# Seven block products in the second MLP product of a fused attention and MLP kernel

## The chip, the core and the metric

The kernel runs on one core of a Trainium2 chip. The metric is the device time of one execution in microseconds (us): a median of 360.05 over 3 runs (360.02 to 360.05). Five engines work side by side, each on its own queue of instructions in order: TensorE (PE, matmuls), VectorE (DVE), ScalarE (ACT), GpSimd (POOL) and SyncE (SP, which only issues DMAs here). Sums of matmuls are kept in PSUM, which has eight banks of 128 x 512 f32; all other tiles are in SBUF.

## What is computed

```python
scores = scale * q @ k^T + decay          # 8 batches x 8 heads, 576 positions, head size 64; causal
attn   = softmax(scores)
x      = (attn @ v), heads side by side   # 4608 tokens x 512
h      = x @ w_in                         # 512 -> 2048
g      = h - tanh(h)
out    = g @ w_out                        # 2048 -> 512, f32
```

`decay` is the difference of two running sums of log f.

## The kernel before

**Attention** goes by pairs of heads: 8 batches of 4 pairs make 32 pairs, `p` = 0 to 31, in a loop with one more turn for what trails. A pair has seven score tiles (`TILES`, 0 to 6; tile 3 is the small one, 128x128, the others up to 128x512). For each, `scores` runs matmuls into one of two PSUM banks (`ps_sc`, line 286), ScalarE takes the exponential into SBUF (`e`, for tile 3 `el`, line 295), and GpSimd clears what lies above the diagonal (line 305). A pair's product with v (`values`, line 317) runs in the following pair, after its tile 2; VectorE divides by the row sums (`rs`, `xn`, lines 324 to 326), and `turn` has two DMA transposes on SyncE's queue (lines 340 and 342) write the result to `XR`, the MLP's input, after tile 3.

**q and k** must have the head's dimension on partitions. The first three batches are transposed on TensorE (`trans`, line 224) and copied by VectorE. From batch `FAR` = 3 on, GpSimd issues loads of blocks of 128 positions (`load_block`, line 86), SyncE issues five DMA transposes into `TQ` and five into `TK` (`turn_block`, line 91), and four copies each of 64 x 1152 (`place`, line 94) move them to `QT` and `KT`, of which there are two sets that take turns by batch. The table `LOADS` says after which tile of which pair each of these is issued; `p0` is the first pair of the batch before the one that is loaded.

**The MLP** goes by nine units of 512 tokens. A step of `mlp1` is four matmuls of 512 columns into a PSUM bank (line 356), tanh on ScalarE (361), and an addition on VectorE that writes `gt`, g in 16 bits (364). There are 16 such steps, one for each 128 of the 2048 columns. A step of `mlp2` is four of the 16 matmuls of 512 columns that make 128 tokens of output (372); after the fourth, ScalarE copies the bank to `ost` (376) and SyncE stores it (378). A unit has 16 steps of each kind. Both use `ps_m`, a ring of three banks; `ps_av` has two, `ps_tr`, for transposes, one.

**The order.** For all engines but ScalarE the program's order is the queue's order (`manual_schedule`). ScalarE's order is free after the start: a scheduler sets it when the kernel is built. The main loop puts MLP steps between the attention's steps, by `take` steps a pair, spread evenly:

```python
take = 0 if p < NPAIR else 2 if p == NPAIR else 7 if p == NPAIR + 1 else 6 if p <= 2 * NPAIR else 8
```

What is left when attention ends (some two units) runs alone at the end.

Of the kernel before, what the change touches and what calls it, by code (L numbers as in the profile page):

```python
# [8 lines left out]
FP32 = mybir.dt.float32  # L9
FP16 = mybir.dt.float16  # L10
# [7 lines left out]
FAR = 3  # L18
# [3 lines left out]
def kernel(  # L22
# [23 lines left out]
    NFT = DFF // P  # L46
    NCH = DM // P
    UW = 512
    NU = NT // UW

    cst = ctx.enter_context(tc.tile_pool(name="cst", bufs=1))
# [1 line left out]
    wpl = ctx.enter_context(tc.tile_pool(name="wpl", bufs=1))  # L53
    aex = ctx.enter_context(tc.tile_pool(name="aex", bufs=10))
    fin = ctx.enter_context(tc.tile_pool(name="fin", bufs=3))
    gtp = ctx.enter_context(tc.tile_pool(name="gtp", bufs=NFT + 6))
    tmp = ctx.enter_context(tc.tile_pool(name="tmp", bufs=2))
    PSUM = bass.MemoryType.PSUM
    ps_sc = ctx.enter_context(tc.tile_pool(name="ps_sc", bufs=2, space=PSUM))
    ps_av = ctx.enter_context(tc.tile_pool(name="ps_av", bufs=1, space=PSUM))  # L60
# [2 lines left out]

    win = wpl.tile([P, NCH, DFF], FP16)
    wout = wpl.tile([P, NFT, DM], FP16)
    RING = 4 * S
    XR = wpl.tile([P, NCH, RING], FP16)

# [20 lines left out]
    def turn_block(dst, src, b, n):  # L89
        pn = min(P, S - n * P)  # L90
        nc.sync.dma_start_transpose(out=dst[:, :, n * P:n * P + pn], in_=src[b % 2][0:pn, n, :])

    def place(dst, src, b, a, c):
        nc.vector.tensor_copy(out=dst[b % 2][0:D, 2 * c + a:2 * c + 3 + a:2, 0:S], in_=src[a * D:(a + 1) * D, c:c + 2, :])

    def load_v_rest(b):
        nc.gpsimd.dma_start(out=vn[b % 2][0:S % P, NJ - 1, :, 0:D],
# [7 lines left out]
        nc.gpsimd.dma_start(out=vn[b % 2][:, n, h0:h1, 0:D],  # L105
                            in_=v[b, h0:h1, n * P:(n + 1) * P, :].rearrange("h p d -> p h d"))

    lf = cst.tile([NH, S], FP32)
    nc.sync.dma_start(out=lf, in_=f.rearrange("b h s -> (b h) s"))
    load_qk(qn, q, 0, 0, 2)  # L110
    load_qk(kn, k, 0, 0, 2)
# [5 lines left out]
                            fill=1.0, base=0, pattern=[[-1, P]], channel_multiplier=1)  # L117
    load_qk(qn, q, 0, 2, 4)
    load_qk(kn, k, 0, 2, 4)
    ones16 = cst.tile([NH, S], FP16)  # L120
    sel = cst.tile([P, 2], FP16)
    dec = cst.tile([P, PITCH], FP16)
    nc.vector.memset(ones16, 1.0)
    minus16 = cst.tile([2 * H, S], FP16)
    nc.vector.memset(minus16, -1.0)
    late = cst.tile([P, P], FP16)
    nc.vector.memset(late, 0.0)
# [13 lines left out]
    nc.vector.memset(vn[0][D:P, NJ - 1, :, :], 0.0)  # L141
    nc.vector.memset(vn[0][:, :, :, D:VW], 1.0)
    nc.scalar.activation(out=lf, in_=lf, func=AF.Ln)
    cum = cst.tile([NH, S], FP32)
    nc.vector.tensor_tensor_scan(out=cum, data0=ones16, data1=lf, initial=0.0,  # L145
                                 op0=ALU.mult, op1=ALU.add)
    chi = dec[0:NH, 0:S]
# [46 lines left out]
    for b in range(2, B):  # L194
        p0 = (b - 1) * NPAIR
        for n in range(NJ - 1):
            LOADS.setdefault((p0 + 1, n), []).append(lambda b=b, n=n: load_v_block(b, n, 0, H))
        LOADS.setdefault((p0 + 1, 4), []).append(lambda b=b: load_v_rest(b))
        LOADS.setdefault((p0, 0), []).append(lambda b=b: load_aug(b))
        if b < FAR:  # L200
            continue
        for n in range(NJ):
            LOADS.setdefault((p0 - 1, n), []).append(lambda b=b, n=n: load_block(qb, q, b, n))
            LOADS.setdefault((p0, n), []).append(lambda b=b, n=n: load_block(kb, k, b, n))
            LOADS.setdefault((p0, 4), []).append(lambda b=b, n=n: turn_block(TQ, qb, b, n))
            LOADS.setdefault((p0 + 1, 4), []).append(lambda b=b, n=n: turn_block(TK, kb, b, n))
        for n, (dst, src) in enumerate(((QT, TQ), (KT, TK))):
            for a in range(2):
                for c in (0, 2):
                    LOADS.setdefault((p0 + 3, 2 * n + a), []).append(lambda b=b, dst=dst, src=src, a=a, c=c: place(dst, src, b, a, c))  # L210

    E, XN, GT, M2 = {}, {}, {}, {}

    def trans(b, c, src, dst, early, copies, split=False):
        pn, g3 = S // NT6, NT6 // 2
# [126 lines left out]
        nc.sync.dma_start_transpose(out=XR[:, c, r0 + S - D:r0 + S], in_=xn[D:P, NJ - 1, :])  # L342

    HP = {}

    def mlp1(u, ft, part=None):
        if part != 1:
            HP[(u, ft)] = ps_m.tile([P, UW], FP32, tag="m", name="hps")
        hps = HP[(u, ft)]
        t0 = u * UW % RING  # L350
        parts = [(0, t0, min(UW, RING - t0))]
        if t0 + UW > RING:
            parts.append((RING - t0, 0, t0 + UW - RING))
        for o, t, n in parts:
            for ci in {None: range(NCH), 0: range(NCH - 1), 1: (NCH - 1,)}[part]:
                nc.tensor.matmul(out=hps[:, o:o + n], lhsT=win[:, ci, ft * P:(ft + 1) * P],  # L356
                                 rhs=XR[:, ci, t:t + n], start=(ci == 0), stop=(ci == NCH - 1))
        if part == 0:
            return
        th = tmp.tile([P, UW], FP32, tag="th", name="th")  # L360
        nc.scalar.activation(out=th, in_=hps, func=AF.Tanh, scale=-1.0)  # L361
        gt = gtp.tile([P, UW], FP16, tag="gt", name="gt")
        GT[(u, ft)] = gt
        nc.vector.tensor_tensor(out=gt, in0=hps, in1=th, op=ALU.add)  # L364

    def mlp2(u, s):
        m, part = divmod(s, 4)
        if part == 0:
            M2[u] = ps_m.tile([P, DM], FP32, tag="m", name="ops")
        ops = M2[u]  # L370
        for ft in range(part * 4, part * 4 + 4):
            nc.tensor.matmul(out=ops, lhsT=GT[(u, ft)][:, m * P:(m + 1) * P], rhs=wout[:, ft, :],  # L372
                             start=(ft == 0), stop=(ft == NFT - 1))
        if part == 3:
            ost = tmp.tile([P, DM], FP32, tag="ost", name="ost")
            nc.scalar.activation(out=ost, in_=ops, func=AF.Copy)  # L376
            r0 = u * UW + m * P
            nc.sync.dma_start(out=out[r0:r0 + P, :], in_=ost)

    def unread(n):  # L380
        idle = ps_tr.tile([P, UW], FP32, tag="tr", name="idle")
# [33 lines left out]
    def att_items(p):  # L415
        def put(fn, *args):
            items.append((lambda: fn(*args), True))

        items = []
        here = pairs[p] if p < len(pairs) else None  # L420
        before = pairs[p - 1] if 0 < p <= len(pairs) else None
        after = pairs[p + 1] if p + 1 < len(pairs) else None
        early = p < NPAIR
        for ti in range(len(TILES)):
            if here and (p > 0 or ti > 1):
                put(scores, *here, ti)
            if p == 1 and ti == 6:
                items.append((lambda: const_rows(1), False))
                items.append((lambda: load_aug(1), False))
            if early and p > 0 and ti in (0, 6):  # L430
                put(unread, 2)
            if p == 1 and ti == 3:
                put(last)
            for load in LOADS.get((p, ti), ()):
                items.append((load, False))
            at_q, at_k = (1, 3) if p == 0 else (0, 1) if early else (0, 2) if p == NPAIR else (0, 3 if p == 2 * NPAIR else 2)
            if ti == at_q and after and after[0] < FAR:
                put(trans, *after, qn, QT, early, "VV")
            if p == NPAIR:
                if ti in (3, 4):  # L440
                    put(mlp1, 0, ti - 3, 1)
            if ti == at_k and after and after[0] < FAR:
                put(trans, *after, kn, KT, early, "VV")
            if p == NPAIR:
                if ti == 1:
                    put(turn, *pairs[p - 2])
                    put(values, *before)
                    put(mlp1, 0, 0, 0)
                elif ti == 2:
                    put(mlp1, 0, 1, 0)  # L450
                    put(turn, *before)
            elif early and ti in (2, 3) and before:
                put(values, *before, (ti - 2,))
            elif not early and ti == 2 and before:
                put(values, *before)
            if p < NPAIR:
                if ti == 1 and p > 1:
                    put(turn, *pairs[p - 2])
            elif p > NPAIR and ti == 3:
                put(turn, *before)  # L460
        return items

    mlp = [(fn, u, s) for u in range(NU) for fn in (mlp1, mlp2) for s in range(NFT)]
    mlp = mlp[2:]
    at = 0
    FOUR = {PE, mybir.EngineType.Pool, mybir.EngineType.SP, mybir.EngineType.DVE}
    with tc.manual_schedule(engines=FOUR | {mybir.EngineType.Activation}):
        start()
    with tc.manual_schedule(engines=FOUR):
        bulk()  # L470
        for p in range(len(pairs) + 1):
            b, c = divmod(p, NPAIR)
            items = att_items(p)
            take = 0 if p < NPAIR else 2 if p == NPAIR else 7 if p == NPAIR + 1 else 6 if p <= 2 * NPAIR else 8
            mine = mlp[at:at + take]
            at += take
            first = 14 if p == NPAIR else 0
            given, n = 0, 0
            whole = sum(counts for _, counts in items)
            for emit, counts in items:  # L480
                emit()
                n += counts
                while n > first and given < len(mine) and given * (whole - first) < (n - first) * len(mine):
                    fn, *args = mine[given]
                    fn(*args)
                    given += 1
        for fn, *args in mlp[at:]:
            fn(*args)
# [28 lines left out]
```

## Time and profile before

| | before |
|---|---|
| median of 3 runs | 360.05 us |
| profiled execution | 360.04 us, its span 358.3 us |
| TensorE busy | 348.0 us, 97% |
| ScalarE busy | 220.2 us, 61% |
| VectorE busy | 198.0 us, 55% |
| GpSimd busy | 157.3 us, 44% |
| granted TensorE clock, mean | 0.999 |
| matmuls of the first MLP product (L356) | 640, 140.3 us |
| matmuls of the second MLP product (L372) | 576, 138.3 us |
| score matmuls (L286), values matmuls (L317, f16 tiles e) | 384, 77.7 us; 896, 33.8 us |
| exponentials (L295, e) | 192, 600 ns each |
| g additions (L364) | 144, 689 ns each |

The profile is of one execution; its span is from the first instruction to the last, and the device time lies 1.7 us above it. Matmuls overlap in the pipeline, so a group's busy time is more than what it takes on the chain: the pace is read from the chain that ended last. Idle time of an engine off that chain costs nothing by itself.

### The profile page before, as it was taken

The page shows a single profiled execution, that of the slowest core. Times are in us where ns is not written, and L with a number is a line of the kernel's source. Part 1 is how long each engine was busy: PE and PEld are TensorE (multiplying, and loading weights), DVE is VectorE, ACT ScalarE, POOL GpSimd, SP SyncE. Part 2 cuts the span into 40 slices and gives each one's busy share as a digit, 9 for nine tenths or more (in the row PEclk, how much of TensorE's full clock was granted, in tenths as well). Part 3 has the DMA queues.
Part 4 walks back from the last instruction along what each step waited for, and adds up shares of the span by engine and source line. Part 5 has one row for each costly group of instructions (what it writes and reads, how often), then busy time and mean ns, then how long its engine had stood idle before and what let it go on. Part 6 is the DMA issues. An engine that isn't in the chain of part 4 may idle for free.

```text
span 358.3 us, 7650 instructions
## 1 busy us (share of the span) xinstructions
PE 348.0 (97%) x2869; PEld 193.2 (54%) x2869; DVE 198.0 (55%) x344; ACT 220.2 (61%) x417; POOL 157.3 (44%) x319
## 2 busy tenths in 40 slices
PE   8988999999999999999999999999999999999995
PEld 7476545555555555555557865555555544444442
DVE  6599887568851676157815781478137513802810
ACT  5687775467755885578557865786568624614721
POOL 8974645764476537652766277623222210000000
PEclk9999999999999999999999999999999999999999
DMA  9999999999499939995999899980320021011002
GB/s 109 153 168 199 195 201 130 156 163 140 56 103 172 158 75 85 148 201 87 81 169 169 90 74 157 182 105 18 93 75 16 18 75 63 0 59 59 2 33 84
DMA packets 140744, 38.74 MB, mean 108 GB/s; under 512 B 128116, under 2 KB 135012, under 8 KB 140708
## 3 DMA queue, kind: packets, MB, share of 16 engines
q0 software_dynamic: 92480, 18.39, 67.1%
q1 hardware_dynamic: 48228, 19.88, 26.4%
q8 instruction: 22, 0.36, 0.5%
q14 instruction: 14, 0.11, 0.1%
HBM read 36.85 MB, written 9.44 MB: 129 GB/s over the span
## 4 chain that ended last, share of the span: by engine, by line
PE 88%; ACT 4%; DVE 4%; issue 1%; DMA 1%; POOLq 0%; POOL 0%; ACTq 0%
PE ops L372 34%; PE hps L356 31%; PE ps L286 11%; PE av L317 8%; ACT e L295 3%; PE t L224 1%; DVE gt L364 1%; DVE QT L237 1%; ACT th L361 1%; PE ps L289 1%; DMA lf<-in_f_dram 1%; PE ps L257 1%; PE ps L255 0%; DVE KT L237 0%; DVE cum L145 0%
## 5 line engine op out<-in xcount | busy, mean ns | idle before, releaser
L356 PE MATMUL hps<-XR,win 128*128 128x512 f16 (+1 forms) x640 | 140.3, 357 | 0.7 <-ACT XR L338 0.7
L372 PE MATMUL ops<-wout,gt 128*128 128x512 f16 x576 | 138.3, 378 | 0.0
L295 ACT ACTIVATE e<-ps 128x512 f16<-128x512 f32 x192 | 110.9, 600 | 41.2 <-PE ps L286 35.9
L364 DVE TENSOR_TENSOR gt<-hps,th 128x512 f16<-128x512 f32 x144 | 98.8, 689 | 59.8 <-ACT th L361 59.3
L361 ACT ACTIVATE th<-hps 128x512 f32<-128x512 f32 x144 | 86.8, 603 | 34.2 <-PE hps L356 33.9
L305 POOL TENSOR_SCALAR_AFFINE_SELECT e<-e 128x128 f16<-128x128 f16 x168 | 56.8, 339 | 79.8 <-ACT e L295 77.3
L356 PEld LDWEIGHTS <-win 128*128 128x128 f16 x640 | 57.9, 97 | 49.4 <-issue 0.3
L372 PEld LDWEIGHTS <-gt 128*128 128x128 f16 x576 | 52.1, 97 | 54.8 <-issue 0.5
L286 PE MATMUL ps<-QT,KT 67*128 67x64 f16 (+5 forms) x384 | 77.7, 276 | 1.8 <-ACT e L295 1.3
L286 PEld LDWEIGHTS <-KT 67*128 67x128 f16 (+1 forms) x384 | 36.8, 98 | 36.1 <-issue 1.5
L376 ACT ACTIVATE ost<-ops 128x512 f32<-128x512 f32 x36 | 21.5, 597 | 39.2 <-PE ops L372 39.2
L324 DVE TENSOR_SCALAR rs<-av 128x10 f32<-128x10 f32 x32 | 5.2, 162 | 67.1 <-PE av L317 65.5
L317 PEld LDWEIGHTS <-e 128*128 128x128 f16 x896 | 32.2, 97 | 6.3 <-POOL e L305 0.7
L317 PE MATMUL av<-vn,e 128*128 128x65 f16 x896 | 33.8, 193 | 0.6 <-POOL e L305 0.6
L105 POOL DMA_DIRECT2D vn<-in_v_dram x32 | 27.9, 876 | 9.8 <-DMA win<-in_moe_w_in_dram 4.1
L326 DVE TENSOR_TENSOR xn<-av,rs 128x640 f16<-128x640 f32 x32 | 26.4, 825 | 1.1
L305 POOL TENSOR_SCALAR_AFFINE_SELECT el<-el 128x128 f16<-128x128 f16 x28 | 8.5, 304 | 33.5 <-ACT el L295 32.9
L237 DVE COPY QT<-t 64x576 f16<-64x576 f16 x22 | 17.6, 801 | 9.7 <-PE t L224 9.5
L86 POOL DMA_DIRECT2D qn<-in_q_dram x25 | 21.5, 861 | 2.7 <-issue 2.7
L86 POOL DMA_DIRECT2D kn<-in_k_dram x25 | 21.1, 846 | 2.3 <-issue 2.3
L237 DVE COPY KT<-t 64x576 f16<-64x576 f16 (+1 forms) x26 | 19.5, 749 | 2.4 <-PE t L224 2.1
L295 ACT ACTIVATE el<-ps 128x128 f16<-128x128 f32 x32 | 8.8, 276 | 16.4 <-PE ps L286 16.3
(60 smaller groups left out, 144.1 us busy)
## 6 DMA issues: line engine op xcount, KB each, us to landing
out_dram<-ost SPq DMA_DIRECT2D x36, 256.0 KB
vn<-in_v_dram POOLq DMA_DIRECT2D x24, 128.0 KB, 5.5
qn<-in_q_dram POOLq DMA_DIRECT2D x20, 128.0 KB, 3.8
kn<-in_k_dram POOLq DMA_DIRECT2D x20, 128.0 KB, 4.8
win<-in_moe_w_in_dram POOLq DMA_DIRECT2D x2, 1024.0 KB, 14.8
wout<-in_moe_w_out_dram POOLq DMA_DIRECT2D x2, 1024.0 KB, 14.5
XR<-xn SPq DMA_TRANSPOSE x56
vn<-in_v_dram POOLq DMA_DIRECT2D x12, 64.0 KB, 5.0
```

What stands on the lines that cost most here:

```text
L86: nc.gpsimd.dma_start(out=dst[b % 2][0:pn, n, :].rearrange("p (h d) -> p h d", h=H), in_=src[b, :, n * P:n * P + pn, :].rearrange("h p d - ...
L105: nc.gpsimd.dma_start(out=vn[b % 2][:, n, h0:h1, 0:D], in_=v[b, h0:h1, n * P:(n + 1) * P, :].rearrange("h p d -> p h d"))
L237: nc.vector.tensor_copy(out=to, in_=of)
L286: nc.tensor.matmul(out=ps[:, col:col + n], lhsT=KT[b % 2][0:rows, h, j * P:(j + 1) * P], rhs=QT[b % 2][0:rows, h, i0:i0 + n], start=not ow ...
L295: nc.scalar.activation(out=e[:, lo:hi], in_=ps[:, lo:hi], func=AF.Exp, scale=qscale)
L305: nc.gpsimd.affine_select(out=view, in_=view, compare_op=ALU.is_ge, fill=0.0, base=0, pattern=pat, channel_multiplier=-1)
L317: nc.tensor.matmul(out=av[:, a, ib, :], lhsT=E.pop((b, c, a, j, ib)), rhs=vn[b % 2][:, j, 2 * c + a, 0:D + 1], start=(j == 0), stop=(j == ib))
L326: nc.vector.tensor_tensor(out=xn.rearrange("p i (a d) -> p a i d", a=2), in0=av[:, :, :, 0:D], in1=rs.to_broadcast([P, 2, NJ, D]), op=ALU. ...
L356: nc.tensor.matmul(out=hps[:, o:o + n], lhsT=win[:, ci, ft * P:(ft + 1) * P], rhs=XR[:, ci, t:t + n], start=(ci == 0), stop=(ci == NCH - 1))
L361: nc.scalar.activation(out=th, in_=hps, func=AF.Tanh, scale=-1.0)
L364: nc.vector.tensor_tensor(out=gt, in0=hps, in1=th, op=ALU.add)
L372: nc.tensor.matmul(out=ops, lhsT=GT[(u, ft)][:, m * P:(m + 1) * P], rhs=wout[:, ft, :], start=(ft == 0), stop=(ft == NFT - 1))
```

## The change

Units 0 and 1 keep the plain second product. Units 2 to 8 split g (512 tokens x 2048) and w_out (2048 x 512) into halves both ways and make the four blocks of the output from seven products of blocks, in Winograd's form of Strassen's scheme. `STEPS` lists them: each is two matmul chains of eight with 256 columns. Four sums of blocks of g (`sums`, S1 to S4) are made on VectorE in 16 bits, in four pieces each; three differences of blocks of w_out and one more, in place, are made once (`weights`, in pairs 11 to 13). The banks are combined by two ScalarE copies kept in SBUF (`m1`, `m7`), one ScalarE copy that is stored, and five VectorE operations; a unit has four stores of 256 x 256, and the last unit splits its last one.

The MLP's ring gets a fourth bank (`ps_tr`) from pair 12 on and the two score banks when attention is over (`widen`). g lies in two buffers instead of 22; some work tiles of the start lie in `TQ` and `TK`. `take` becomes 7 and 8 in turn from pair 13 on, and two MLP steps go ahead of the last values product.

For batches 4 to 7, q's loads, q's turn and k's are issued one pair sooner (q's loads two tiles later within it). `place` runs on ScalarE for q and on VectorE for k, at slots from `(p0, 4)` to `(p0 + 2, 1)` instead of pair `p0 + 3`; for batch 3 the slots are `(p0 + 2, 5)` to `(p0 + 3, 5)`.

```diff
+    NK = NFT // 2
+    HU = UW // 2
+    HE = DM // 2
+    PLAIN = 2
-    gtp = ctx.enter_context(tc.tile_pool(name="gtp", bufs=NFT + 6))
+    gtp = ctx.enter_context(tc.tile_pool(name="gtp", bufs=2))
...
-    def place(dst, src, b, a, c):
-        nc.vector.tensor_copy(out=dst[b % 2][0:D, 2 * c + a:2 * c + 3 + a:2, 0:S], in_=src[a * D:(a + 1) * D, c:c + 2, :])
+    def place(dst, src, b, a, c, eng="V"):
+        to, of = dst[b % 2][0:D, 2 * c + a:2 * c + 3 + a:2, 0:S], src[a * D:(a + 1) * D, c:c + 2, :]
+        if eng == "A":
+            nc.scalar.activation(out=to, in_=of, func=AF.Copy)
+        else:
+            nc.vector.tensor_copy(out=to, in_=of)
...
+        e = 0 if b == FAR else 1
         for n in range(NJ):
-            LOADS.setdefault((p0 - 1, n), []).append(lambda b=b, n=n: load_block(qb, q, b, n))
-            LOADS.setdefault((p0, n), []).append(lambda b=b, n=n: load_block(kb, k, b, n))
-            LOADS.setdefault((p0, 4), []).append(lambda b=b, n=n: turn_block(TQ, qb, b, n))
-            LOADS.setdefault((p0 + 1, 4), []).append(lambda b=b, n=n: turn_block(TK, kb, b, n))
-        for n, (dst, src) in enumerate(((QT, TQ), (KT, TK))):
-            for a in range(2):
-                for c in (0, 2):
-                    LOADS.setdefault((p0 + 3, 2 * n + a), []).append(...)
+            LOADS.setdefault((p0 - 1 - e, n + 2 * e), []).append(lambda b=b, n=n: load_block(qb, q, b, n))
+            LOADS.setdefault((p0 - e, n), []).append(lambda b=b, n=n: load_block(kb, k, b, n))
+            LOADS.setdefault((p0 - e, 4), []).append(lambda b=b, n=n: turn_block(TQ, qb, b, n))
+            LOADS.setdefault((p0 + 1 - e, 4), []).append(lambda b=b, n=n: turn_block(TK, kb, b, n))
+        parts = [(dst, src, a, c) for dst, src in ((QT, TQ), (KT, TK)) for a in range(2) for c in (0, 2)]
+        if b == FAR:
+            spots = [(p0 + 2, 5), (p0 + 2, 6)] + [(p0 + 3, ti) for ti in (0, 1, 2, 3, 4, 5)]
+        else:
+            spots = [(p0, 4), (p0, 6), (p0 + 1, 0), (p0 + 1, 2), (p0 + 1, 4), (p0 + 1, 5), (p0 + 1, 6), (p0 + 2, 1)]
+        for spot, (dst, src, a, c) in zip(spots, parts):
+            LOADS.setdefault(spot, []).append(lambda ...: place(dst, src, b, a, c, "A" if dst is QT else "V"))
...
+    RINGS = [[ps_m], [ps_m, ps_m, ps_m, ps_tr], [ps_m, ps_m, ps_m, ps_tr, ps_sc, ps_sc]]
...
+        if u >= PLAIN:
+            if ft in (3, 6, 9, 12):
+                sums(u, "S3", ft // 3 - 1)
...
+    SUMS = {"S3": ("A11", "A21", ALU.subtract), "S2": ("A22", "S3", ALU.subtract),
+            "S1": ("S2", "A11", ALU.add), "S4": ("A12", "S2", ALU.subtract)}
...
+    STEPS = [("A11", B11, "x"), ("S3", B12, "y"), ("A12", B21, "x"), ("S2", W2, "y"),
+             ("S1", W1, "v"), ("A22", W4, "z"), ("S4", B22, "v")]
+    AFTER = {0: (("S2", 0),), 1: (("S2", 1), ("S2", 2)), 2: (("S2", 3), ("S1", 0)), 3: (("S1", 1),), 4: (("S1", 2),),
+             5: (("S1", 3),), 6: (("S4", 0),), 7: (("S4", 1),), 8: (("S4", 2),), 9: (("S4", 3),)}
+
+    def mlp2(u, s):
+        n, m = divmod(s, 2)
+        lhs, rhs, to = STEPS[n]
...
+        for kt in range(NK):
+            nc.tensor.matmul(out=ps[:, m, :], lhsT=LHS[lhs](u, kt // 4)[:, kt % 4, m * P:(m + 1) * P],
+                             rhs=rhs[:, kt, :], start=(fresh and m == 0 and kt == 0),
+                             stop=((m == 1 or ends) and kt == NK - 1), skip_group_check=True)
...
+        for name, i in AFTER.get(s, ()):
+            sums(u, name, i)
...
+        if lhs == "A11":
+            M2["m1"] = copy(kept("m1"))
+        elif lhs == "S3":
+            M2["m7"] = copy(kept("m7"))
+        elif lhs == "A12":
+            give(0, 0, copy)
+        elif lhs == "S2":
+            M2["u3"] = plus(M2["m1"], kept("u3"))
+            nc.vector.tensor_tensor(out=M2["m7"], in0=M2["u3"], in1=M2["m7"], op=ALU.subtract)
+        elif lhs == "S1":
+            give(1, 1, plus, M2["u3"])
+        elif lhs == "A22":
+            give(1, 0, plus, M2["u3"])
+        else:
+            give(0, 1, plus, M2["m7"])
...
-            at_q, at_k = (1, 3) if p == 0 else (0, 1) if early else (0, 2) if p == NPAIR else (0, 3 if p == 2 * NPAIR else 2)
+            at_q, at_k = (1, 3) if p == 0 else (0, 1) if early else (0, 2) if p == NPAIR else (0, 3)
...
+    TAKE = (0, 0, 0, 0, 2, 7, 6, 6, 6, 8, 8, 8, 8)
...
-            take = 0 if p < NPAIR else 2 if p == NPAIR else 7 if p == NPAIR + 1 else 6 if p <= 2 * NPAIR else 8
+            take = TAKE[p] if p < len(TAKE) else 8 - (p - len(TAKE)) % 2
+            if p == 3 * NPAIR:
+                widen(1)
...
+        widen(2)
```

In `mlp2`, `copy` is a ScalarE copy out of the bank, `plus` a VectorE addition to the bank, and `give` stores the result.

## Prediction

> **What bounds the kernel now.** I read the page first, then the chain that ended last.
>
> ```profile
> span 358.3 us, 7650 instructions
> PE 348.0 (97%) x2869; PEld 193.2 (54%) x2869; DVE 198.0 (55%) x344; ACT 220.2 (61%) x417; POOL 157.3 (44%) x319
> PE 88%; ACT 4%; DVE 4%; issue 1%; DMA 1%; POOLq 0%; POOL 0%; ACTq 0%
> ...
> 191.62 1.75 PE hps L356 x16
> ...
> 327.06 13.81 PE hps L356 x64
> 340.87 13.83 PE ops L372 x64
> ```
>
> The last three lines are the chain in order of time (start, us, what). TensorE is the chain: 64 matmuls of 512 columns take 13.81 us, 0.2158 us each, back to back, and 16 of 256 columns, in the unit that wraps round the ring, take 1.75 us, 0.1094 each. Every matmul loads its own weights in both, so half a matmul costs half. Nothing else is scarce over the whole span. In the groups of instructions the attention's score matmuls (L286) wait 1.3 us in all for ScalarE. So fewer columns shorten the span one for one, as long as TensorE stays unbroken; the question is what breaks it.
>
> Time zero below is 181.24, where the values product ends in pair 20. Three timelines of that stretch decide the case: SyncE's queue, TensorE, and ScalarE's groups (busy us, mean ns).
>
> ```profile
> 182.76 1.29 SPq L340 DMA_TRANSPOSE XR<-xn  x1
> 184.11 1.21 SPq L342 DMA_TRANSPOSE XR<-xn  x1
> 185.85 0.34 SPq L378 DMA_DIRECT2D out_dram<-ost  x1
> 186.28 6.47 SPq L91 DMA_TRANSPOSE TQ<-qn  x5
> ...
> 186.06 0.68 PE L286 MATMUL ps<-QT,KT 67*128 67x320 f16 x3
> 187.44 0.38 PE L286 MATMUL ps<-QT,KT 67*128 67x448 f16 x2
> 188.53 0.38 PE L286 MATMUL ps<-QT,KT 67*128 67x320 f16 x2
> 189.61 0.59 PE L317 MATMUL av<-vn,e 128*128 128x65 f16 x14
> 191.39 0.22 PE L286 MATMUL ps<-QT,KT 67*128 67x64 f16 x2
> ...
> L295 ACT ACTIVATE e<-ps 128x512 f16<-128x512 f32 x192 | 110.9, 600 | 41.2 <-PE ps L286 35.9 <-PE ps L289 4.9
> L295 ACT ACTIVATE el<-ps 128x128 f16<-128x128 f32 x32 | 8.8, 276 | 16.4 <-PE ps L286 16.3
> ```
>
> SyncE issues a turn of q only after the XR turn of the pair, and the five issues alone take 6.47 us. The trace's records of landings put the last of the five, here, at 196.19. From first issue to last landing the five batches took 9.2, 11.4, 10.5, 9.9 and 9.8 us, mean 10.15. TensorE meanwhile goes through a whole pair: tile 1 at 187.44 (6.2 on my clock), tile 3 at 191.39 (10.15).
>
> **What the seven products remove.** A unit had 64 matmuls of 512 columns, 13.81 us; it gets 7 products x 2 x 8 = 112 of 256, 112 x 0.1094 = 12.25. That is 1.56 us a unit, 10.9 us for seven. All of it is on the chain. The last store follows a 128x256 addition; 128x512 takes 689 ns and 128x10 162 ns (rs, L324), so about 420 instead of the copy's 597: 0.2 us off the end.
>
> **What they add on VectorE.** 16 sums of 128x512 f16 a unit, and five combinations that read f32. The combinations are gt's kind: 5 x 0.69 = 3.45. For a sum the rows bound the cost at 0.69 (gt, L364, half of it f32) and 0.16 (rs, 10 columns). I take 0.44, the quickest copy of 16-bit data within SBUF (QT<-TQ, 64x1152, 0.443 at least), nearest in types and memories: 7.0 us. A batch of four pairs then asks VectorE for 11.0 (gt) + 7.0 + 3.45 + 4 x 1.2 (rs, reciprocal, xn) + 2.2 (KT copies) = 28.5 us, of 35.3 that TensorE needs (36.9 before, less 1.56): hidden. At 0.69 the two units at the end, with no attention between, are short: twelve sums and two combinations stand before the addition that frees the bank of the last product, which then starts some 1.2 us late in each, 2.5 us in all; that widens the range only. The Trainium skill ("VectorE: DVE Perf Modes", perf-mode tier table) lets tensor_tensor on 16-bit SBUF data run at twice the plain rate, which I estimate at (151 + 256)/0.96 = 424 ns a sum; no run here shows one, and by it the 2.5 us would be nothing. The eight weight differences (128x1024) lie in pairs 11 to 13, where VectorE has few gt; even at twice 0.69 they cost no chain time.
>
> **Edits that I cost at nothing.** Four banks replace three in the ring, so the MLP waits no more than now (0.7 us). Two buffers replace 22 for g, but a unit's first addition comes after the last product of the unit before on TensorE's own order. Stores stay four a unit, of 1 KB rows. POOL's loads of q move two pairs up and those of k one, past POOL's own selects; POOL is at 44%. The work tiles that now lie in TQ and TK, the later k transposes of pairs 5 to 7, and the two MLP steps ahead of the last values touch no queue that is late.
>
> **The copies of q, moved to ScalarE.** This is the expensive part. Four 64x1152 copies a batch go from VectorE, three pairs after their turn, to ScalarE. The el and e rows give (600-276)/384 = 0.84 ns a column, so 1.14 us each (VectorE's own copy, 0.56, is the lower bound). ScalarE's order is not written by hand after the start, and in the built kernel it is, for pair 16 (and alike for 20 and 24):
>
> ```
> e (tile 0) ; QT<-TQ, waits for the five transposes ; e (tile 1) ; ost copy ; e (tile 2) ; QT<-TQ x2 ; el (tile 3) ; QT<-TQ ; e (tile 4)
> ```
>
> The first copy stands before tile 1, earlier than the slot (tile 4) in which the program names it. The turn is now issued one pair sooner, in the pair of my clock, behind its XR turn: without the out store SyncE starts it at 4.1, and it has landed at 4.1 + 10.15 = 14.2. ScalarE comes to the copy at 6.7. Behind it are queued every exponential of the pair. TensorE has two score banks: tile 2 still runs, the values too, but tile 3 needs the bank of tile 1, whose exponential waits.
> - Copy 14.2 to 15.35, e of tile 1 to 15.95, tile 3 at 16.0 instead of 10.15: TensorE stands 5.85 us.
> - Then ost to 16.5, e to 17.0, two copies to 19.2, el to 19.5, copy to 20.6, e of tile 4 to 21.2. Tile 5 waits for el, tile 6 for that e, the next pair's tile 0 for the one after, 21.75; undisturbed it starts at 13.55 (three Strassen steps of 0.875 and the tiles). The loss is 8.2 us a batch.
>
> Batch 4 (pair 12) has two copies before el and two behind, and its turn waits for an out copy too: landed 15.4, tile 5 stands from 13.05 to 18.0, the next tile 0 goes from 14.4 to 21.3: 6.9 us. Batch 3 keeps its old turn; its first copy, behind tile 4 of pair 9, waits about 1 us and pushes one tile: 2 us, bounds 0 and 4.
>
> Sum: 3 x 8.2 + 6.9 + 2 = 33.5 us added. The profiled execution took 360.04 (span 358.3 and 1.74 around it), as the median 360.05: 360.0 - 10.9 - 0.2 + 33.5 = 382.4, say **382**.
>
> **The clock in the pauses.** Windows over the end of the trace (the granted clock is the third number from the end):
>
> ```profile
> 354.70:357.50 2.80, 0.00 (x0) 0.00 (x0) 0.00 (x0) 0.60 (x1) 0.00 (x0) 1.00 0.25 94
> 357.80:358.30 0.50, 0.00 (x0) 0.00 (x0) 0.00 (x0) 0.00 (x0) 0.00 (x0) 0.50 0.00 0
> ```
>
> It halves some 3 us after the last matmul. Pauses of 5 us should show it too; steps then take 1.75 us at first, which the lines above bear because the tiles wait for ScalarE anyway.
>
> **The rivals.**
> - **The copies find their data (faster, 349).** Against the forecast, the five transposes would land by 8.3 rather than 14.2: a copy and an exponential (1.7 us) then still end before tile 3. That is the point from which it decides. Then only the columns count: 360.0 - 11.1 = 349. For it speaks that today's landings share the DMA engines with POOL's loads (busy share 0.9 to 2.6 per us); against it that the issue alone ends at 10.6. What is left is that I misread the order or who waits. Chance 0.08.
> - **The clock stays down (slower still, 394).** TensorE restarts in fits, at half rate, and the pauses between tiles keep it there into the next pair: about 6 us of work at half rate a batch, of which half is not under ScalarE's delay, 3 x 4 = 12 us more. In the first 6 us of this span the clock came up only after matmuls from 1.13 to about 6.2. The Trainium skill ("TensorE: Matmul & The Clock Gate", Part 1) has windows of 3.4 us, one idle to halve and one busy to restore, which the 3 us above agree with; by it a batch loses 1 us or less here, since one window of steady work ends it. Chance 0.07.
> - **Half-width products save nothing (392).** 112 matmuls would cost 13.8 us; the chain's 1.75 for 16 speaks against. Chance 0.02.
>
> **How the numbers follow.** The forecast has 0.82. Its own bounds: a landing at 9.2 or 11.4 moves each of four batches by 1.1 us; copies at 0.56 save 2.3 a batch; batch 3 gives 2 either way; dear sums add 2.5; a clock that lingers adds some us. Together 369 to 393, which leaves out the 349 and the far clock case. Measurement of this kernel can tell about 0.2%. Faster holds 0.08; within 0.2% would need the stalls to equal the gain, 0.01; the rest, 0.91, is slower.
>
> **What would show it.** Right: in the changed profile four holes of about 5 us in TensorE, 35 us apart, each ended by an exponential; ScalarE idle before QT<-TQ, released by a DMA; clock below 1.00 there; 112 matmuls in 12.25 us in the last unit. Wrong: ScalarE's copies waiting under 2 us each time, or TensorE waiting for VectorE's sums.

## The result and the profile after

| | before | after |
|---|---|---|
| median | 360.03 us (360.01 to 360.05, 4 runs) | 381.68 us (378.73 to 382.63, 4 runs) |
| profiled execution | 360.04, span 358.3 | 382.29, span 380.6 |

The ratio is 1.0587, with a 95% interval from 1.0527 to 1.0647: 21.65 us slower, where 22 was forecast. First the page of the changed kernel: span, busy time, the granted clock by slices, the chain by engine, and the row of the copies of q (busy us, mean ns, idle before). The two lines behind it are of the kernel before: its clock, and its copies of q.

```profile
span 380.6 us, 8472 instructions
PE 351.5 (92%) x3205; PEld 230.7 (61%) x3205; DVE 252.2 (66%) x480; ACT 235.1 (62%) x430; POOL 162.0 (43%) x319
PEclk9999999997997799989998999879999999999999
PE 58%; ACT 9%; DVE 8%; SPq 7%; DMA 6%; issue 5%; POOL 4%; ACTq 0%; DVEq 0%; POOLq 0%
L106 ACT ACTIVATE QT<-TQ 64x1152 f16<-64x1152 f16 x20 | 22.8, 1156 | 23.5 <-DMA TQ<-qn 23.4
```

```profile
PEclk9999999999999999999999999999999999999999
L94 DVE COPY QT<-TQ 64x1152 f16<-64x1152 f16 x20 | 11.5, 613 | 0.2
```

TensorE held 88% of the chain and now holds 58%. The largest single part of what came in its place is the route of q: by lines, SyncE's issues of q's turns have 7% of the chain, their DMAs 4%, and ScalarE's copies 3%. ScalarE stands 23.4 us ahead of those copies, and one takes 1156 ns there, where VectorE took 613. The clock has dips from slice 10 to 27, where before had none. The waits (us in total, times, longest), and the one of the kernel before that goes with the second:

```profile
ACT QT L106 <- DMA TQ<-qn: 23.4, 5, 6.3
PE ps L314 <- ACT e L323: 17.5, 11, 4.3
PE ps L314 <- ACT el L323: 2.8, 1, 2.8
```

```profile
PE ps L286 <- ACT e L295: 1.3, 3, 0.5
```

Five waits, one a batch, and TensorE's score matmuls (L314, before L286) wait 20.3 us for exponentials instead of 1.3. The timelines of SyncE, ScalarE and TensorE at pair 16 show one of them whole. On the prediction's clock, zero is here at 148.7, where the values product in pair 15 ends:

```profile
153.44 7.01 SPq L101 DMA_TRANSPOSE TQ<-qn  x5
...
154.26 1.08 ACT L323 ACTIVATE e<-ps 128x512 f16<-128x512 f32 x2
161.65 1.16 ACT L106 ACTIVATE QT<-TQ 64x1152 f16<-64x1152 f16 x1 [6.32 <-DMA TQ<-qn]
162.72 0.57 ACT L323 ACTIVATE e<-ps 128x512 f16<-128x512 f32 x1
...
157.99 1.04 PE L452 MATMUL ops<-W,sq 128*128 128x256 f16 x8
163.35 0.26 PE L314 MATMUL ps<-QT,KT 67*128 67x64 f16 x2 [4.32 <-ACT e L323]
163.42 1.90 PE L452 MATMUL ops<-W,sq 128*128 128x256 f16 x8
```

SyncE issues the five transposes from 153.44; the record of landings has the last at 161.55. ScalarE has been idle since 155.3 with the exponential of tile 1 behind the copy, and TensorE's tile 3 waits 4.32 us for that exponential's bank. The step of eight matmuls after it takes 1.90 instead of 1.04: half clock. At the end, where no copies of q stand, the change does what the prediction counted; this is the chain of the last full unit (start, us, what):

```profile
324.21 13.81 PE hps L396 x64
338.02 12.23 PE ops L452 x112
```

### The profile page after: what moved, and what is told of

Read it like the earlier page. It is cut to its first block, busy times and chain, and to the rows that moved or that the text cites. A ratio compares the mean times of both kernels' runs of the same rounds, so it can differ in the third digit from the quotient of the medians.

```text
span 380.6 us, 8472 instructions
## 1 busy us (share of the span) xinstructions
PE 351.5 (92%) x3205; PEld 230.7 (61%) x3205; DVE 252.2 (66%) x480; ACT 235.1 (62%) x430; POOL 162.0 (43%) x319
## 4 chain that ended last, share of the span: by engine, by line
PE 58%; ACT 9%; DVE 8%; SPq 7%; DMA 6%; issue 5%; POOL 4%; ACTq 0%; DVEq 0%; POOLq 0%
PE hps L396 22%; PE ops L452 17%; PE ps L314 7%; SPq L101 7%; PE av L345 5%; ACT e L323 4%; PE ops L430 4%; DMA TQ<-qn 4%; DVE gq L405 3%; ACT QT L106 3%; POOL e L333 2%; POOL qn L96 2%; DMA TK<-kn 1%; ACT th L401 1%; PE t L252 1%
## 5 line engine op out<-in xcount | busy, mean ns | idle before, releaser
L396 PE MATMUL hps<-XR,win 128*128 128x512 f16 (+1 forms) x640 | 143.7, 362 | 1.6 <-DVE gq L405 0.9
L323 ACT ACTIVATE e<-ps 128x512 f16<-128x512 f32 x192 | 110.3, 597 | 27.9 <-PE ps L314 21.9
L405 DVE TENSOR_TENSOR gq<-hps,th 128x512 f16<-128x512 f32 x144 | 98.0, 688 | 29.5 <-ACT th L401 27.9
L333 POOL TENSOR_SCALAR_AFFINE_SELECT e<-e 128x128 f16<-128x128 f16 x168 | 61.1, 366 | 102.1 <-ACT e L323 100.5
L314 PE MATMUL ps<-QT,KT 67*128 67x64 f16 (+5 forms) x384 | 80.9, 284 | 21.7 <-ACT e L323 17.5
L314 PEld LDWEIGHTS <-KT 67*128 67x128 f16 (+1 forms) x384 | 37.6, 100 | 45.8 <-issue 20.4
L452 PEld LDWEIGHTS <-gq 128*128 128x128 f16 x560 | 53.4, 98 | 11.1 <-issue 1.5
L452 PE MATMUL ops<-wout,gq 128*128 128x256 f16 x448 | 55.1, 272 | 0.6 <-DVE ost L458 0.6
L106 ACT ACTIVATE QT<-TQ 64x1152 f16<-64x1152 f16 x20 | 22.8, 1156 | 23.5 <-DMA TQ<-qn 23.4
L430 PE MATMUL ops<-wout,gq 128*128 128x512 f16 x128 | 35.8, 409 | 0.0
L452 PE MATMUL ops<-W,sq 128*128 128x256 f16 x224 | 31.8, 299 | 0.0
L354 DVE TENSOR_TENSOR xn<-av,rs 128x640 f16<-128x640 f32 x32 | 26.4, 825 | 1.3 <-DVE rs L353 0.3
L452 PEld LDWEIGHTS <-sq 128*128 128x128 f16 x224 | 23.3, 107 | 5.2 <-issue 0.8
L470 DVE TENSOR_TENSOR ost<-ops,u 128x512 f32<-128x512 f32 x14 | 9.6, 688 | 25.1 <-PE ops L452 25.1
## 6 DMA issues: line engine op xcount, KB each, us to landing
win<-in_moe_w_in_dram POOLq DMA_DIRECT2D x2, 1024.0 KB, 14.2
```

The lines of the kernel that those rows point to most:

```text
L106: nc.scalar.activation(out=to, in_=of, func=AF.Copy)
L314: nc.tensor.matmul(out=ps[:, col:col + n], lhsT=KT[b % 2][0:rows, h, j * P:(j + 1) * P], rhs=QT[b % 2][0:rows, h, i0:i0 + n], start=not ow ...
L323: nc.scalar.activation(out=e[:, lo:hi], in_=ps[:, lo:hi], func=AF.Exp, scale=qscale)
L333: nc.gpsimd.affine_select(out=view, in_=view, compare_op=ALU.is_ge, fill=0.0, base=0, pattern=pat, channel_multiplier=-1)
L405: nc.vector.tensor_tensor(out=GQ[(u, i)][:, half, kt, :], in0=hps, in1=th, op=ALU.add)
L430: nc.tensor.matmul(out=ops, lhsT=GQ[(u, ft % NK // 4)][:, ft // NK, ft % 4, m * P:(m + 1) * P], rhs=wout[:, ft, :], start=(ft == 0), stop= ...
```

## The experiments

The time of a pair, below, is from the end of the values product in that pair to the end of the next one.

The theory: the products save what they remove, and all that is lost comes from ScalarE's copies of q, which stand in its queue ahead of exponentials and wait for the transposes. The rivals: half-width products cost something elsewhere; the half clock, not the wait, makes the loss; the copies' own time on ScalarE does.

### The change taken apart

The seven products with loads, turns and copies of q and k as they were (VectorE, pair `p0 + 3`):

```diff
-            LOADS.setdefault((p0 - e, 4), []).append(lambda b=b, n=n: turn_block(TQ, qb, b, n))
+            LOADS.setdefault((p0, 4), []).append(lambda b=b, n=n: turn_block(TQ, qb, b, n))
...
-            LOADS.setdefault(spot, []).append(lambda ...: place(dst, src, b, a, c, "A" if dst is QT else "V"))
+                    LOADS.setdefault((p0 + 3, 2 * n + a), []).append(lambda ...: place(dst, src, b, a, c))
```

> The seven products alone: loads, turns and copies of q and k stand where they stood before, all copies on VectorE in pair p0 + 3. Theory: 10.9 us of matmuls less, and 1 to 2 for the later k transposes; but VectorE now has 12.3 us of work in that pair of 9.2 (2.8 g, 0.4 S3, 1.2 xn, 8 sums x 0.43, 8 copies x 0.55), so up to 3 us a batch come back: 347 to 362 us, no wait on TQ. Rival 2 (products and sums cost the time): 375 or more.

And the kernel before with the new loads, turns and copies alone:

> The kernel before with the new loads, turns and copies of q and k alone, plain second product; the scheduler puts ScalarE's copies in pairs 12, 16, 20 and 24 two behind tile 2 and two behind tile 3's el. Theory: ScalarE waits 4 to 6 us per batch for the last transpose, TensorE loses 6 to 8 us a batch and as much in pairs 9 and 10: 360 + 30 = 390, 383 to 397 us, four or five stretches at half clock. Rival 2 (products and sums): 358 to 362.

Measured: products alone 347.92 (347.70 to 348.06, ratio 0.9663, 0.9648 to 0.9677); copies alone 394.02 (393.12 to 397.13, ratio 1.0971, 1.0921 to 1.1021). Products -12.1, copies +34.0, sum +21.9; both together measured +21.65. So they add up, and neither hides in the other. Waits of the two, products alone first:

```profile
PE ps L309 <- ACT e L318: 1.5, 4, 0.5
```

```profile
ACT QT L96 <- DMA TQ<-qn: 20.2, 5, 5.2
PE ps L295 <- ACT el L304: 11.3, 4, 3.7
PE ps L295 <- ACT e L304: 10.1, 13, 2.5
```

The plain second product has five such waits too, one a batch, so they do not come from Strassen's scheme.

### The turn earlier, and ScalarE's order by hand

If the wait is the cost, q's turn ahead of the pair's XR turn should remove it while ScalarE keeps the copy in the same place:

```diff
-            LOADS.setdefault((p0 - e, 4), []).append(lambda b=b, n=n: turn_block(TQ, qb, b, n))
+            LOADS.setdefault((p0 - e, 1), []).append(lambda b=b, n=n: turn_block(TQ, qb, b, n))
...
-    with tc.manual_schedule(engines=FOUR):
+    with tc.manual_schedule(engines=FOUR | {mybir.EngineType.Activation}):
```

with the copies named where ScalarE had them, `(p0, 0), (p0, 2), (p0, 2), (p0, 3)`.

> The turns of q are issued after tile 1 of their pair instead of tile 4, ahead of the XR turns in SyncE's queue; ScalarE's queue is written by hand in the very order that the changed kernel has in pairs 16, 20 and 24 (first copy behind tile 0, two behind tile 2, one behind tile 3). Theory (ScalarE's queue stands behind a copy whose data has not landed): the last landing comes some 6 us after the values' end, before ScalarE comes to the copy at 6.7; waits of the copies under 1 us each, no clock record of 0.5 in the middle, 349 to 356 us. Rival 1 (the four copies themselves, 4.6 us of ScalarE in half a pair, cost the time): 4 to 6 us a batch stay, 368 to 378. Rival 2 (the seven products and their sums cost it): 375 or more.

Measured: 366.39 (365.83 to 369.48, ratio 1.0194, 1.0152 to 1.0236), which misses the expectation by 10.

```profile
ACT QT L106 <- DMA TQ<-qn: 11.0, 4, 4.0
```

The wait fell by 12.4 us and the time by 15.3 (by 13.4 against the order by hand with the turns left in place, 379.75, below), so most of the loss goes with the wait; but the wait did not go away. Issued earlier, the turns took longer: 12.5, 12.3 and 13.6 us from first issue to last landing in pairs 16, 20 and 24, against 8.1, 7.6 and 7.9 in the changed kernel. I put this down to q's own loads just ahead of them, though no run shows that apart, and for batch 4, in pair 12, the turn was hardly longer, 8.6 against 8.0. In pairs 16, 20 and 24 they landed 7.5 to 10.2 us after the values instead of 12.0 to 12.9, and ScalarE comes to the copy at about 6.7. Pair 14, where no copy of q stands, is 3.8 longer than with products alone; this version does not tell why.

Next, ScalarE's queue in the program's order, with all slots as the change names them (only the second hunk above):

> ScalarE's queue is in the program's order, all else as in the changed kernel, so a batch's copies stand behind tiles 4 and 6 and the next pair's 0 and 2. Theory: the data lands at about 12.9 us after the values' end, ScalarE comes to the first copy at about 12, so each batch waits about 1 us instead of 5 to 6 and TensorE loses 1 to 2 us a batch: 351 to 358 us. Rival 1 (the copies' own time): 370 or more, as the same 4.6 us of copies are there. Rival 2 (products and sums): 375 or more.

Measured: 374.34 (373.61 to 375.16, ratio 1.0398, 1.0381 to 1.0414), again far off. The waits, then VectorE's and TensorE's timelines in pair 18:

```profile
DVE KT L108 <- DMA TK<-kn: 15.1, 4, 5.0
PE ps L314 <- ACT e L323: 12.8, 12, 3.4
PE hps L396 <- DVE gq L405: 7.8, 9, 2.4
ACT QT L106 <- DMA TQ<-qn: 4.9, 3, 2.4
```

```profile
174.18 0.45 DVE L108 COPY KT<-TK 64x1152 f16<-64x1152 f16 x1 [4.99 <-DMA TK<-kn]
...
175.28 1.84 PE L396 MATMUL hps<-XR,win 128*128 128x512 f16 x4 [2.36 <-DVE gq L405]
```

ScalarE's wait is down from 23.4 to 4.9, and a wait of the same kind has come up on VectorE: the copy of k waits for its turn, the additions of g stand behind it, and TensorE waits for their bank. Of the 26.4 us that this version takes over products alone, 16.3 are in pairs 14, 18, 22 and 26, where k's copies hold the queue. In the changed kernel these copies did not wait: for batches 5 to 7 k's last transpose had landed 0.4 to 0.8 us before the first of them, which TensorE's stop for q in the pair before gave it the time to do. So there are two copies named too early, and the first hid the second.

With the copies of k a pair later, and then with those of q later too:

```diff
-            spots = [(p0, 4), (p0, 6), (p0 + 1, 0), (p0 + 1, 2), (p0 + 1, 4), (p0 + 1, 5), (p0 + 1, 6), (p0 + 2, 1)]
+            spots = [(p0, 4), (p0, 6), (p0 + 1, 0), (p0 + 1, 2), (p0 + 2, 1), (p0 + 2, 2), (p0 + 2, 4), (p0 + 2, 5)]
...
+            spots = [(p0, 6), (p0 + 1, 0), (p0 + 1, 1), (p0 + 1, 2), (p0 + 2, 1), (p0 + 2, 2), (p0 + 2, 4), (p0 + 2, 5)]
```

> Like e3_hand_order, with the copies of k of batches 4 to 7 in pair p0 + 2 (behind tiles 1, 2, 4, 5) instead of p0 + 1. In e3 VectorE stood 15.1 us in four waits for k's turn. Theory (the wait went from ScalarE's copies of q to VectorE's copies of k): those 15.1 us vanish, and with them about what pairs 14, 18, 22 and 26 lost: 355 to 360 us. Rival (the copies' own time on ScalarE and VectorE): little changes, 370 or more, as the same copies are made.

> Like e8_hand_k_later, and the copies of q one slot later too (behind tile 6 of pair p0 and tiles 0, 1, 2 of the next). Theory: no copy waits for data; what is left over e1 (347.9) is the copies' time on ScalarE in pairs that also have g to make: 348 to 354 us. Rival: 370 or more.

Measured: 361.97 (360.57 to 362.83, ratio 1.0046, 1.0033 to 1.006) with k later, 12.4 less than with ScalarE's order alone, which bears out that k's wait was the larger part there; 357.87 (356.90 to 358.23, ratio 0.9936, 0.9918 to 0.9955) with both. The waits with both later:

```profile
PE ps L314 <- ACT e L323: 8.9, 16, 1.6
DVE KT L108 <- DMA TK<-kn: 1.4, 1, 1.4
ACT QT L106 <- DMA TQ<-qn: 1.0, 1, 1.0
```

Both came out above what was expected, the first by 2 us, the second by 4. Pair 12 makes the difference between them: with k later alone, q's first copy there still waits 2.4 us, the clock halves, and the pair takes 15.77 instead of 10.62. With both later the copies find their data, the clock is 1.0, and the kernel is still 10 us slower than with the copies on VectorE. Of these 10, 7.4 are score matmuls that wait for exponentials (8.9 against 1.5), 16 short waits: twenty copies of 1156 ns are 23 us in ScalarE's queue, between exponentials that the two score banks wait for. That they alone make the rest of the 10 is argued; the order of ScalarE's queue and the slots of the turns differ too.

### The clock in the pauses

Is the loss the wait, or the half clock that follows it? A control has the order that the scheduler chose, written out by hand; the other kernel has dummy matmuls of 128 columns added in the five waits, into an unused part of the values' bank:

```diff
+    FILL = {(10, 0): 40, (12, 5): 45, (16, 3): 60, (20, 3): 45, (24, 3): 50}
+    def fill(p, n):
+        av = AV[pairs[p - 2 if p == 10 else p - 1]]
+        for i in range(n):
+            nc.tensor.matmul(out=av[:, 1, 352:480], lhsT=warm, rhs=warm, start=True, stop=True)
```

> The changed kernel with ScalarE's queue written by hand, q's copies in the slots that the scheduler gave them (four places in the queue differ by one step). Every theory: as the changed kernel, 376 to 385 us. It is the control for the next kernel, and says whether the place in the queue, not the scheduler's other choices, makes the time.

> The control, and in the five long waits of TensorE (ahead of tile 0 of pair 10, tile 5 of pair 12, tile 3 of pairs 16, 20 and 24) 40, 45, 60, 45 and 50 matmuls of 128 columns on constants into an unused part of the values' bank, 2.2 to 3.4 us of work each, so that TensorE is not idle for long and its clock stays up; they compute nothing. If the waits alone make the time (my sum of the prediction, which gave the clock 0.3 us a batch): 0 to 2 us less than the control. If the clock has a share of its own (steps of 1.7 us instead of 0.87 after the waits in pairs 10, 12 and 24, where little else holds them): 5 to 9 us less, and no record of 0.5 in the middle. If the fill outlasts a wait: slower than the control.

Measured: control 379.75 (378.94 to 380.74, ratio 1.0548, 1.0523 to 1.0573), filled 379.83 (378.12 to 381.52, ratio 1.0549, 1.0513 to 1.0585). TensorE in pair 16, the control first:

```profile
160.40 0.27 PE L314 MATMUL ps<-QT,KT 67*128 67x64 f16 x2 [4.48 <-ACT e L323]
160.48 1.90 PE L452 MATMUL ops<-W,sq 128*128 128x256 f16 x8
```

```profile
157.78 3.51 PE L502 MATMUL av<-warm 128*128 128x128 f16 x60 [0.51 <-DVE xn L354]
161.12 0.22 PE L314 MATMUL ps<-QT,KT 67*128 67x64 f16 x2
161.19 1.04 PE L452 MATMUL ops<-W,sq 128*128 128x256 f16 x8
...
164.32 0.38 PE L314 MATMUL ps<-QT,KT 67*128 67x448 f16 x2 [1.00 <-ACT el L323]
```

The step after the pause takes 1.04 instead of 1.90, and TensorE then waits 1.00 for ScalarE, which the half clock had covered. Pair 16 takes 14.28 us instead of 15.84, but its last transpose also landed 0.8 sooner (12.1 after the values against 12.8), so only some 0.8 of the 1.6 are the clock's. In pair 12 the last transpose landed 0.8 later than in the control, the filling did not keep the clock up (matmuls in 47% of the window, and half clock for 6.8 us in both), and 1.4 were lost. Pair 20 did not move; there the clock stays up in the control too. Pair 24 lost 0.3 with a landing 0.3 later, though its clock now stays up. So the half clock costs the control 0.8 us at most in a batch where the filling removed it, and the waits make most of its loss; for pair 12 this stays open.

The control differs from the changed kernel in one place that matters. In pair 9, behind q's first copy, the changed kernel has a tanh ahead of the exponential, the control has it behind. The control's tile waits 1.97 us and the clock stays up; in the changed kernel the tile there waits 2.58 and the clock halves:

```profile
85.11 0.58 PE L314 MATMUL ps<-QT,KT 67*128 67x512 f16 x1 [2.58 <-ACT e L323]
85.49 1.91 PE L396 MATMUL hps<-XR,win 128*128 128x512 f16 x4
```

Pairs 9 and 10 take 25.95 us in the changed kernel and 22.91 in the control. Here TensorE, with eight MLP steps a pair, was the one behind: up to the next values product it waits for nothing more, and three steps take 1.76 to 1.91 us instead of 1.03. So I give the clock some 2.5 us of the 3.0, an estimate; the rest is the longer pause.

### Two small terms

The prediction costed the later k transposes of pairs 5 to 7 at nothing. The kernel before with these alone:

```diff
-            at_q, at_k = ... else (0, 3 if p == 2 * NPAIR else 2)
+            at_q, at_k = ... else (0, 3)
```

> The kernel before with one edit: the transposes of k in pairs 5 to 7 stand behind tile 3 instead of tile 2 (at_k), as in the changed kernel. Both kernels of mine with that edit reach pair 8 1.8 us sooner than the kernel before, and the profile before has TensorE's transposes wait 1.9 us for VectorE's copies of q out of the one bank that they share (PE t from DVE QT, and 3.2 us on the weights' side). If that edit is the reason: 358.0 to 358.6 us. If the gain comes from another part (the MLP's buffers, the work tiles): 359.8 to 360.3.

Measured: 359.34 (359.32 to 359.53, ratio 0.9977, 0.9967 to 0.9987), 0.7 faster, between the two ranges. At the end of pair 8 it is 1.8 ahead, as in the changed kernel, but part of that is work put off: it has done one MLP step (0.87) and six transposes of k (0.26) fewer. Pair 10 makes up for both and takes 10.41 instead of 8.64; a wait for an addition of g (0.27) and one for an exponential (0.15) fall there too. What is left of the 1.8, some 0.7, is the gain.

The last product's second half waits for a bank, `DVE ost` (L458), for 0.57 us in the changed kernel:

```profile
375.99 1.03 PE L452 MATMUL ops<-wout,gq 128*128 128x256 f16 x8 [0.57 <-DVE ost L458]
```

The best version of the above, products alone, with the last block in one addition and one store (`ends = False` for the last unit):

> e1 (the seven products with the old copies), and the last unit stores its last block like the others, with one addition and one store, instead of in two halves. In the changed kernel's profile the last eight matmuls wait 0.57 us for the addition that reads the other half of their bank. If that wait sets the end: 0.57 less, 0.27 more for the longer addition, 347.4 to 347.8. If the store of twice the size costs as much: 347.8 to 348.3.

Measured: 347.38 (347.36 to 347.40, ratio 0.9648, 0.9635 to 0.9661), 0.54 less than products alone: the wait of 0.57 went, and the longer addition and store gave almost nothing back. This is the fastest version, 12.7 us faster than before and 34.3 than the changed kernel.

## Why the prediction was right

The total was right, and so was the mechanism: ScalarE's copies of q wait for their transposes and hold up exponentials that TensorE needs. That the total came within 1 us is luck: inside, three terms were off and cancelled, some 6 us too much for batches 5 to 7 against 5 too little for batches 3 and 4, and 1.3 more in pair 14. Measured losses by batch are pair times of the changed kernel against products alone, which has the same matmuls.

- **Products.** Forecast -10.9, from 12.25 us for 112 matmuls; the chain shows 12.23. Products alone gave -12.1; 0.7 of that is the k transposes, an edit that I had costed at nothing. What is left, 0.5, or 1.0 with the 0.54 of the next point, I did not trace.
- **The last store.** Forecast -0.2 for a smaller last piece; it cost 0.54, since the piece's addition keeps the last matmuls from their bank.
- **Sums on VectorE.** Taken at 0.44 and hidden. The rows:

```profile
L422 DVE TENSOR_TENSOR gq<-gq 128x512 f16<-128x512 f16 x28 | 13.2, 470 | 0.0
L422 DVE TENSOR_TENSOR sq<-gq 128x512 f16<-128x512 f16 x28 | 9.9, 416 | 0.0
```

  The other two kinds take 424 and 435 ns, so the mean of all is 0.436 us. The estimate of 424 from the Trainium skill ("VectorE: DVE Perf Modes", perf-mode tier table) agrees with all but the 470. The 2.5 us that dear sums would have cost did not come.
- **Batches 5 to 7.** Forecast 8.2 each; measured 6.5, 5.6 and 6.9. The step that was off is the landing: I had the turn at 10.15 us, the mean of before, and so the landing 14.2 after the values; it took 8.1, 7.6 and 7.9, and landed at 12.9, 12.0 and 12.3. Why the turns were quicker than before no run shows. The order on ScalarE and who waits were as said: tile 3 stood 4.3, 3.4 and 3.7 instead of 5.85.
- **Batch 4.** Forecast 6.9, measured 8.4. The turn landed at 13.4 after the values instead of 15.4, but the pair went on at half clock for 10.2 us, most of it beside ScalarE's delay; how much of the 8.4 is the clock's stays open. Another 1.3 us were lost in pair 14, where a wait for an exponential follows VectorE's last weight difference and the copies of k; the prediction had nothing there.
- **Batch 3.** Forecast 2, bounds 0 to 4; measured 5.7. The copy waited 1.7 where I had said about 1, with exponentials behind it, and the pause of 2.58 us halved the clock where TensorE was the one behind.
- **Sum.** Forecast +33.5; copies alone gave +34.0, and the changed kernel less products alone +33.8.
- **The clock.** The sum gave it nothing, and the rival 12 us more. In batch 3 it is some 2.5. In batches 5 to 7 the pairs take 0.6, 0.0 and 0.5 more than with the pauses filled; the 0.6 is all a later landing, and with the landings allowed for, the 0.5 becomes 1.0. For batch 4 it stays open. So my price was too low by some 3.5 us, batch 4 apart, and the rival's was too high by more.
- **The rivals.** "The copies find their data, 349": the wait can be removed, but with the copies on ScalarE that gives 357.9; 349 needs them on VectorE. It left out that the copy takes 1156 ns of ScalarE's queue also when nobody waits. "Half-width products save nothing" is refuted by 347.92.
- **What it would show.** The holes came in pairs 12, 16, 20 and 24, each ended by an exponential, with ScalarE idle before `QT<-TQ`; they were 2.8 to 4.3 us rather than 5, and 41 to 44 us apart rather than 35, the loss itself being part of the period. A fifth came in pair 9.
- **A reading that was wrong without consequence.** POOL's loads of q move up by one pair less two tiles, not by two pairs.

## What to carry to other kernels

An operation that waits for a DMA costs what stands behind it in its engine's queue, so read its place in the built order, not the slot in the program, and set that against the measured landing, not the issue. When one such wait is taken away, look for the next that it covered: here k's copies behind q's. An engine with idle time over the whole span (ScalarE, 61%) may still have none at the place where a copy is put; VectorE, which became busier (77%), took the same copies at no cost that shows in the time.

## What the runs showed of the hardware

**The clock is decided in fixed windows of 3.413 us, by the busy share.** Every stretch at half clock, but for the one that the end of a trace cuts off, lasts 3.413, 6.827 or 10.240 us, and within a run all begin on one grid of 3.413 us. I laid the union of the matmul records (whose ends are modelled) over this grid for all the kernels run. At full clock, windows with matmuls in 43% of them or less were all followed by half clock, windows of 57% or more never were, and between 46 and 56% both occur. Full clock came back after a window at half clock with 90% or more, and not after one with 89% or less. So the pause of 2.58 us halved the clock, because it left its window 43% busy, and the control's pause of 1.97 us did not: its windows were 61 and 81% busy. The Trainium skill ("TensorE: Matmul & The Clock Gate", Part 1) has a free-running window of 3413 ns, which agrees; it halves the clock after an idle window, where here a window less than half busy was enough.

**Landing time of the same five transposes** went from 7.6 to 13.6 us: 7.6 to 8.1 for batches 4 to 7 of the changed kernel (9.3 for batch 3), 9.2 to 11.4 in the kernel before, and, issued ahead of the XR turn, 12.3 to 13.6 for batches 5 to 7 but 8.6 and 9.5 for batches 4 and 3. So it is not set by the place in SyncE's queue alone.
